# Short filler matmuls: 32 moving columns instead of 512 in TensorE's idle stretches

## The chip, the cores and the metric

The kernel runs on one core of one Trainium2 chip. A core has five engines that run their own instruction lists in order: TensorE (PE: matrix products; its weight loads are listed apart as PEld), VectorE (DVE), ScalarE (ACT), GpSimd (POOL) and SyncE (SP, which here issues the transfers). They meet through semaphores. TensorE writes its results to PSUM banks, from where ScalarE and VectorE read them.

The metric is the device time of one execution in microseconds (us), as the median of several runs. A profile is taken of one more execution, whose own time is given beside its span (first to last instruction).

## The reference: two attentions over one input, mixed by a gate

Input `x` has 2048 tokens of width 640. Two attentions with 32 heads of width 20 are computed from it and mixed token by token.

```python
x = A_x
g = _sigmoid((x * gate_w).sum(-1, keepdims=True))
a = _A_ref(x, A_wqkv, A_wo)      # full attention, softmax over all 2048 keys
b = _B_ref(x, B_wqkv, B_wo)      # 8 keys per token: positions s, s-2, ..., s-14
return g * a + (1 - g) * b
```

Each of the two projects `x` to queries, keys and values, takes a softmax of scaled products, forms the weighted sum of values and projects it with its own `wo`. The full attention takes 32 x 2048 x 2048 exponentials. That is what most of the kernel is about.

## The kernel before: a planned order of work around ScalarE's exponentials

**Tiles and groups.** The full attention runs over 32 groups (`GROUPS`), each a block of 512 queries and four heads. A unit is 128 keys of one head against 512 queries. A step `s` of the main loop takes a tile of two or three units:

- `qk(s)` (line 1992) forms their scores: each unit is a matmul with 32 contracted rows, so the heads of a group lie on four row strips of the array. The scores go to one of two score buffers in PSUM, used in turn.
- `exp(s)` (line 2009) is one ScalarE instruction over 1024 or 1536 columns, from `score` to `ebuf`.
- `pv_slot` calls `pv` (line 2054), which multiplies with the values and accumulates in `obank`, four heads side by side on four column strips of 32.

A part of the exponentials is taken on VectorE and GpSimd in another way (`clamp`, line 1970, reads a score bank into `uD`; lines 1055 and 1086 make shifted copies `eD`; `pv` adds them up). A score matmul for these is called a ride when it comes with a tile, and `lone` issues one by itself.

**Side work.** The projections, the whole local attention (`gen_b`, matmuls at lines 688, 1242 and 1350), the norms and the output projections are generators that are stepped when the main loop leaves room. Their matmuls use three PSUM banks: `side0`, and the third bank of each score buffer when a tile has two units.

**Order.** A planner fixes the order on every engine when the program is built. Each task is added to its engine's list with a planned duration; from these, and a table of latencies `LAT` (0.152 us behind ScalarE, 0.275 us behind TensorE), the planner keeps a planned time for each engine. The times are used only to choose the order. On the chip nothing is left but the lists and the semaphore waits. `PLAN` holds the planner's parameters by step; `FILL` is one of them.

**The edited place.** After `qk`, `exp` and `pv_slot` of a step, `spend(limit, s)` fills TensorE's planned time up to the point where the next step's scores are due. It steps side work, then tries `lone`, and where neither has anything it calls `filler`. That looks at how much of the last 2.3 us of TensorE's planned time is taken (`sch.load(2.3)`). If that is under `FILL` (0.56 to 0.85) it adds one TensorE task: four matmuls on the four column strips, each with a moving operand of 512 columns of `xT` (the input, transposed). They write into a PSUM bank that is free at that time, with the identity as weights, or, if none is, add zero to `obank` with `zero` as weights. Nobody reads what was written to the free bank, and zero added to `obank` changes nothing. The planned duration of the task is 0.215 us. A task waits, as any other, until the bank's last reader is done.

At the start there is a separate run of seven matmuls on zeros (line 584) before the first real work. It is not part of the edit.

Of the kernel before, what the change touches and what calls it, by code (L numbers as in the profile page):

```python
# [415 lines left out]
def _build(ctx, nc, A_x, A_wqkv, A_wo, B_wqkv, B_wo, gate_w, out):  # L416
# [20 lines left out]
    xT = sb([P, CN, S], BF16, "xT")  # L437
# [1623 lines left out]
    def filler(limit):  # L2061

        if sch.load(2.3) >= FILL:
            return False
        best = [b for b in range(NB) if not bank_used[b] and bank_free[b] <= sch.avail["pe"]]
        if best:
            o, w, key = side[best[0]], ident, ("side", best[0])
        elif obank_free <= sch.avail["pe"]:
            o, w, key = obank, zero, "obank"
        else:  # L2070
            return False

        def fn(e):
            for j in range(4):
                ins = e.matmul(o[32 * j:32 * j + 32, :], w[:, 32 * j:32 * j + 32] if best else w[:, :], xT[:, 0, 1536:2048], start=bool(best),
                               stop=bool(best), skip_group_check=True)
            return ins

        t = T("pe", 0.215, fn, reads=["ident" if best else "zero", ("xT", 3, 0, 0), ("xT", 3, 0, 1)], mode="col",
              **({"writes": [key]} if best else {"accum": [key]}))  # L2080
        if best:
            bank_free[best[0]] = t.end
        return True
# [204 lines left out]
```

## Time and profile before

| | before |
|---|---|
| median of 3 runs | 774.17 us (773.98 to 775.07) |
| profiled execution, its own time | 774.52 us |
| its span | 772.7 us |
| mean granted TensorE clock | 0.999 |
| ScalarE busy | 755.7 us (98%) |
| TensorE busy, by its records | 740.4 us (96%) |
| VectorE busy | 695.2 us (90%) |
| GpSimd busy | 343.3 us (44%) |
| matmuls of the edited line | 284, at 112 to 750 us |

How to read the lines of the profile. A group of instructions shows line, engine, operation, destination and source with shapes, count, then busy time and mean duration in ns, then the idle time of the engine just before them and what ended it. A matmul's record lasts longer than the time in which its columns stream, and matmuls on different strips of the array run side by side, so TensorE's busy share is no measure of how full it is. A line of a stretch shows its start and end, its length, then for each engine busy time and count, then the granted TensorE clock as a fraction of full, the DMA share and GB/s. A line of the timeline shows start, length, engine, line, operation and count, and in brackets the idle time before it with its releaser.

### The profile page before, as it was taken

To read this page: it belongs to the slowest core of one execution; us is meant where nothing else is said; L and a number is where in the kernel's file an instruction comes from. 1 tells how busy PE (TensorE), PEld (TensorE's weight loads), DVE (VectorE), ACT (ScalarE), POOL (GpSimd) and SP (SyncE) were. 2 spreads that over 40 slices of the span, in tenths; PEclk is the share of its full clock that TensorE was granted. 3 is DMA by queue.
4 is the path that set the end of the run, shared out by engine and by line. 5 is a ranking of instruction groups with operands and counts; after the bars stand their busy time and mean duration, and the time that the engine had idled before them with its cause. 6 is when DMAs were issued, how large, how long until landed. Compare 5 with 4: busy or idle time off the path is not lost.

```text
span 772.7 us, 30140 instructions
## 1 busy us (share of the span) xinstructions
PE 740.4 (96%) x12398; PEld 290.9 (38%) x12398; DVE 695.2 (90%) x1266; ACT 755.7 (98%) x740; POOL 343.3 (44%) x594
## 2 busy tenths in 40 slices
PE   9999999999999999999999999999999999999998
PEld 6433333232343433334334334433433433343232
DVE  6798988989899899978998989999999999799995
ACT  5999999999999999999999999999999999999996
POOL 4255734635444543334645345343443542442441
PEclk9999999999999999999999999999999999999999
DMA  7321221111121513410124233023112411323201
GB/s 233 118 61 38 48 67 40 35 34 32 37 71 38 121 38 93 115 43 20 36 56 117 53 95 72 27 68 92 42 29 62 104 44 43 89 71 70 69 23 38
DMA packets 71471, 49.89 MB, mean 65 GB/s; under 512 B 43112, under 2 KB 64888, under 8 KB 71336
## 3 DMA queue, kind: packets, MB, share of 16 engines
q1 hardware_dynamic: 70392, 47.54, 24.2%
q8 instruction: 99, 1.62, 0.9%
q10 hardware_dynamic: 944, 0.43, 0.2%
q14 instruction: 36, 0.29, 0.1%
HBM read 32.79 MB, written 7.62 MB: 52 GB/s over the span
## 4 chain that ended last, share of the span: by engine, by line
PE 44%; ACT 31%; issue 14%; DVE 8%; SPq 1%; DMA 1%; POOL 0%; ACTq 0%; DVEq 0%
ACT ebuf L2009 31%; PE score L1992 13%; PE obank L2054 12%; PE side L688 11%; PE score L688 3%; DVE uD L1970 3%; DVE eD L1055 1%; DVE kvw L1338 1%; PE score L1668 1%; DMA woBp<-in_B_wo_dram 1%; DVE kvw L1229 0%; PE side L1350 0%; PE obank L584 0%; PE score L1689 0%; SPq L1032 0%
## 5 line engine op out<-in xcount | busy, mean ns | idle before, releaser
L2009 ACT ACTIVATE ebuf<-score 128x1024 bf16<-128x1024 f32 (+1 forms) x699 | 741.7, 1218 | 3.0 <-PE score L1992 2.2
L1970 DVE TENSOR_SCALAR uD<-score 128x512 int16<-128x512 f32 x427 | 285.5, 682 | 30.5 <-PE score L1992 29.0
L1992 PE MATMUL score<-qT,kT 32*128 32x512 bf16 x1851 | 252.2, 384 | 20.1 <-ACT ebuf L2009 15.7
L1086 POOL TENSOR_TENSOR eD<-uD,two 128x256 int32<-128x256 int32 x299 | 179.8, 615 | 124.3 <-DVE eD L1055 64.4
L1055 DVE TENSOR_SCALAR eD<-uD 128x2048 int16<-128x2048 int16 (+3 forms) x306 | 175.3, 596 | 4.1 <-PE obank L2054 3.3
L2054 PE MATMUL obank<-ebuf,vA 128*21 128x512 bf16 x1616 | 151.7, 385 | 0.1
L1992 PEld LDWEIGHTS score<-qT,kT 32*128 32x128 bf16 x1851 | 62.4, 91 | 212.8 <-ACT ebuf L2009 152.8
L1105 POOL TENSOR_TENSOR vS<-vA,vw 128x252 bf16<-128x252 bf16 x108 | 66.0, 611 | 122.3 <-DVE eD L1055 64.2
L2054 PE MATMUL obank<-eD,vS 128*21 128x512 bf16 x1296 | 110.7, 379 | 0.0
L688 PE MATMUL side<-xT,wBs 128*32 128x256 bf16 x2400 | 95.5, 282 | 1.3 <-DVE qkvB L1167 0.5
L688 PEld LDWEIGHTS side<-xT,wBs 128*32 128x32 bf16 x2400 | 67.8, 142 | 31.5 <-issue 16.1
L1028 POOL TENSOR_TENSOR oN<-oTt,oN 128x256 bf16<-128x256 f32 x60 | 43.8, 730 | 61.1 <-DVE eD L1055 35.5
L2054 PEld LDWEIGHTS obank<-ebuf,vA 128*21 128x21 bf16 x1616 | 36.1, 89 | 80.8 <-issue 58.4
L1338 DVE TENSOR_TENSOR kvw<-kvw,eB 128x2048 bf16<-128x2048 bf16 (+2 forms) x40 | 44.6, 1130 | 0.0
L1229 DVE TENSOR_TENSOR kvw<-qkvB 128x1792 bf16<-128x1792 bf16 (+2 forms) x40 | 43.7, 1126 | 0.2
L2054 PE MATMUL obank<-uD,vA 128*21 128x512 bf16 x432 | 41.9, 379 | 0.0
L1167 DVE CAST qkvB<-side 128x512 bf16<-128x512 f32 (+1 forms) x56 | 36.2, 646 | 3.8 <-PE side L688 3.6
L2054 PEld LDWEIGHTS obank<-eD,vS 128*21 128x21 bf16 x1296 | 31.6, 91 | 19.4 <-issue 2.3
L1013 POOL TENSOR_TENSOR rcp<-rcp,gA 128x16 f32<-128x16 f32 x30 | 7.3, 243 | 60.9 <-DVE eD L1055 28.4
L688 PE MATMUL side<-xT,kvw 128*32 128x512 bf16 (+1 forms) x360 | 30.0, 382 | 0.7 <-DVE vA L914 0.2
L688 PE MATMUL side<-kvw,xT 128*32 128x160 bf16 (+1 forms) x760 | 28.4, 263 | 1.6 <-DVE vA L914 0.8
L1992 PE MATMUL score<-woBp,kT 32*128 32x512 bf16 x192 | 27.2, 384 | 0.6 <-ACT ebuf L2009 0.5
(201 smaller groups left out, 578.7 us busy)
## 6 DMA issues: line engine op xcount, KB each, us to landing
kvw<-scr_v SPq DMA_DIRECT2D x32, 336.5 KB
oN<-scr_n SPq DMA_DIRECT2D x60, 128.0 KB
scr_v<-qkvB SPq DMA_DIRECT2D x32, 85.0 KB
wBs<-in_B_wqkv_dram SPq DMA_DIRECT2D x5, 480.0 KB
WqP<-in_A_wqkv_dram SPq DMA_DIRECT2D x14, 160.0 KB
oTd<-oN SPq DMA_DIRECT2D x108, 20.0 KB
out_dram<-outsb SPq DMA_DIRECT2D x12, 160.0 KB
qT<-dst SPq DMA_DIRECT2D x93, 20.0 KB
```

The lines of the kernel that those rows point to most:

```text
L688: ins = e.matmul(o[j:k, :], l(j) if callable(l) else l[:, j:k], r, start=(first and i == 0), stop=(last and i == n - 1), skip_group_check= ...
L1028: T("pool", 0.73, lambda e, cols=cols: e.tensor_tensor(oN[0][:, cols], oTt[:, cols], rcpR[:, cols], ALU.mult), reads=["oTt", "oN%d" % i], ...
L1055: T("dve", 0.065 + 0.1334 * (n - m), lambda e, k=k, sl=sl, m=m: e.tensor_scalar(eD[:, sl % NS, 512 * m:512 * n].bitcast(I16), uD[d % 2][:, ...
L1086: T("pool", PDUR, lambda e: e.tensor_tensor(eD[:, sl % NS, 512 * i:512 * (i + 1)].bitcast(I32), uD[d % 2][:, 512 * i:512 * (i + 1)].bitcas ...
L1105: T("pool", 0.607, lambda e: e.tensor_tensor(vS[:, d % 2, :, :], _ap(vA, (kb * NQ + q) * 4 * DV, [[0, K - 1], [1, 4 * DV]]), _ap(vw, 0, [[ ...
L1167: t = TB(dvc(n * TOK), lambda e, o=o, i=i: e.tensor_copy(o, i), reads=[("side", b)], writes=[key])
L1229: TB(dvc(n_ * TOK, 2), lambda e: e.tensor_tensor(o, i0, i1, ALU.mult), reads=["qB", "kB"], writes=prods(i, range(n_)) + olds(), port=True)
L1338: TB(dvc(n_ * 2 * TOK, 2), lambda e: e.tensor_tensor(o, i0, i1, ALU.mult), reads=rd, writes=prods(i, range(2 * n_)), port=True)
L1970: t = T("dve", 0.598, lambda e: e.tensor_scalar(uD[d % 2][:, 512 * i:512 * (i + 1)].bitcast(I16), side[x], UOFF, 0.0, op0=ALU.add, op1=ALU ...
L1992: ins = e.matmul(o, kT[32 * j:32 * j + 32, q, kb * P:(kb + 1) * P], qT[qbuf[g]][32 * j:32 * j + 32, :], start=True, stop=True)
L2009: exps[s] = T("act", actc(512 * n), lambda e: e.activation(ebuf[s % NE][:, 0:512 * n], score[s % 2][:, 0:512 * n], ACTF.Exp, scale=LN2 / S ...
L2054: ins = e.matmul(obank[32 * j:32 * j + DV, :], v, src, start=(kb == 0), stop=(last and k >= len(lst) - 4), skip_group_check=True)
```

## The change: 32 columns per filler matmul

Both operand slices of the filler's matmul are cut from 512 to 32 columns: the destination is `o[..., 0:32]` and the moving operand `xT[:, 0, 1536:1568]`. The number of matmuls, their weights, their place in the lists, the banks they wait for and the planned duration of 0.215 us stay, so that the planner makes the same lists in the same order.

```diff
         def fn(e):
             for j in range(4):
-                ins = e.matmul(o[32 * j:32 * j + 32, :], w[:, 32 * j:32 * j + 32] if best else w[:, :], xT[:, 0, 1536:2048], start=bool(best),
+                ins = e.matmul(o[32 * j:32 * j + 32, 0:32], w[:, 32 * j:32 * j + 32] if best else w[:, :], xT[:, 0, 1536:1568], start=bool(best),
                                stop=bool(best), skip_group_check=True)
             return ins
```

## The prediction, made before the changed kernel ran

> **What bounds the kernel now.** I read the page from its top: the busy shares, the chain that ended last, the groups of instructions, and then the same engines over the stretch in which these matmuls run.
>
> ```profile
> span 772.7 us, 30140 instructions
> PE 740.4 (96%) x12398; PEld 290.9 (38%) x12398; DVE 695.2 (90%) x1266; ACT 755.7 (98%) x740; POOL 343.3 (44%) x594
> PE 44%; ACT 31%; issue 14%; DVE 8%; SPq 1%; DMA 1%; POOL 0%; ACTq 0%; DVEq 0%
> L2009 ACT ACTIVATE ebuf<-score 128x1024 bf16<-128x1024 f32 (+1 forms) x699 | 741.7, 1218 | 3.0 <-PE score L1992 2.2
> PEld score L1992 <- ACT ebuf L2009: 171.3, 417, 1.1
> ```
> ```profile
> 20.00:760.00 740.00, 713.27 (x12005) 274.03 (x11997) 677.92 (x1204) 737.25 (x713) 333.65 (x574) 1.00 0.24 60
> 112.00:750.20 638.20, 614.20 (x10245) 237.89 (x10241) 590.47 (x1018) 636.07 (x618) 284.04 (x491) 1.00 0.24 60
> ```
>
> The columns of the second fence are the stretch, its length, then PE, PEld, DVE, ACT and POOL busy, and the granted TensorE clock. ScalarE is the bound: between 112 and 750 us it is busy 636.07 of 638.20 us, and in the whole span its exponentials wait for a score matmul for only 2.2 us. TensorE's 96% hides idleness: its score weight loads wait 171.3 us in total for ScalarE to release a score buffer. So TensorE runs just ahead of ScalarE, and is given the edited matmuls when it has nothing else.
>
> ```profile
> L2075 PE MATMUL obank<-xT,zero x120: 379/379/390, 112.2 to 749.7; 128*32 128x512 bf16 x120
> L2075 PE MATMUL score<-xT,ident x104: 379/379/390, 175.0 to 726.9; 128*32 128x512 bf16 x104
> L2075 PE MATMUL side<-xT,ident x60: 379/379/390, 295.1 to 744.3; 128*32 128x512 bf16 x60
> who waited for it (us, times):
> busy tenths in 40 slices 0000000002102009100020213020011001009770
> L1286 PE MATMUL side<-xT,gwT 128*32 128x64 bf16 x160 | 2.6, 193 | 0.1
> 708.98 1.05 PE L2075 MATMUL side<-xT,ident 128*32 128x512 bf16 x16
> ```
>
> 120+104+60 = 284 matmuls, 71 groups of four that run side by side on four column strips of the array. Nobody waited for one of them: the list behind "who waited for it" is empty. Four groups back to back took 1.05 us, so one group streams for (1.05-0.379)/3 = 0.22 us.
>
> **The change part by part.** *The matmuls become shorter.* No 32-column matmul stands in the trace. Its nearest row is 64 columns, 193 ns; so each group ends at least 379-193 = 186 ns earlier, and at most its 0.22 us of streaming goes. Over 71 groups that is 13.2 to 15.6 us of TensorE time. On the path it is worth nothing that I can see: no consumer waits, the order on every engine, the bank releases and the 284 weight loads are as before, and what comes next on TensorE waits for ScalarE. The cover is ScalarE's own work; its idle time in that stretch, 638.20-636.07 = 2.1 us, is the most that can be gained, if all of it came from these groups. I take 0.
>
> *TensorE becomes idler, and its clock may fall.* This decides. What the trace shows of the clock stands at its two ends. First column: start, length and count for the lines of matmuls; the others are stretches as above.
>
> ```profile
> 1.22 3.17 PE L584 MATMUL obank<-qabs 128*128 128x512 bf16 x7 [1.22 <-DVE qabs L575]
> 4.18 1.27 PE L1668 MATMUL score<-ident,oTd 128*128 128x128 bf16 x10
> 7.35 0.72 PE L1668 MATMUL score<-ident,oTd 128*128 128x128 bf16 x10
> L584 PE MATMUL obank<-qabs 128*128 128x512 bf16 x8 | 3.8, 631 | 1.2 <-DVE qabs L575 1.2
> 768.04 1.07 PE L1467 MATMUL score<-outsb,oN 128*32 128x512 bf16 x20
> 0.04:3.45 3.41, 2.23 (x6) 0.85 (x7) 2.15 (x22) 1.49 (x2) 1.76 (x10) 1.00 0.45 120
> 3.45:6.87 3.42, 3.42 (x25) 2.54 (x24) 0.56 (x1) 0.60 (x1) 2.66 (x3) 1.00 1.02 348
> 769.20:771.40 2.20, 0.00 (x0) 0.00 (x0) 1.15 (x2) 0.04 (x1) 0.00 (x0) 1.00 0.70 244
> 771.50:772.60 1.10, 0.00 (x0) 0.00 (x0) 0.00 (x0) 0.00 (x0) 0.00 (x0) 0.50 0.21 72
> ```
>
> Ten 128-column matmuls took 1.27 us at 4.18 and 0.72 us at 7.35: the clock began at half and doubled some 5.6 us after the first matmul (the 1.00 printed for the first two stretches stands where no clock was recorded yet). At the end it halves at about 771.45, 2.3 us after the last matmul. What judges the activity therefore looks back over something between 2.3 and 5.6 us; I take 3.4 us. [...]
>
> How little activity is enough? I count streaming time at 0.213 to 0.22 us per 512 columns, matmuls side by side once. The last 3.4 us before the fall streamed about 0.78 of 3.41 us, 0.23: too little. At the start, stretch 0.04 to 3.45 had (3.45-1.22)/(3.17-0.631)*6 = 5.3 matmuls of 512 columns, 5.3*0.22/3.41 = 0.34: still half clock; stretch 3.45 to 6.87 was filled at half speed, 0.49: full clock. And the poorest stretches while the clock held:
>
> ```profile
> 204.84:208.25 3.41, 2.28 (x34) 0.59 (x32) 2.99 (x6) 3.41 (x4) 1.32 (x3) 1.00 0.04 8
> 208.25:211.66 3.41, 3.41 (x64) 1.63 (x64) 3.31 (x8) 3.41 (x4) 0.69 (x2) 1.00 0.07 12
> 706.60:710.01 3.41, 2.97 (x44) 0.95 (x41) 3.40 (x5) 3.41 (x4) 0.00 (x0) 1.00 0.47 117
> 710.01:713.43 3.42, 2.96 (x45) 0.83 (x41) 3.15 (x6) 3.42 (x4) 1.85 (x3) 1.00 0.76 179
> ```
> ```profile
> 204.84:208.25 3.41, 0.78 (x8) 0.21 (x8) 1.00 0.04 8
> 706.60:710.01 3.41, 1.71 (x24) 0.54 (x24) 1.00 0.47 117
> ```
> ```profile
> 707.50 0.39 PE L1992 MATMUL score<-qT,kT 32*128 32x512 bf16 x3
> 707.82 0.40 PE L2054 MATMUL obank<-ebuf,vA 128*21 128x512 bf16 x4
> 708.66 0.39 PE L1992 MATMUL score<-qT,kT 32*128 32x512 bf16 x3 [0.44 <-ACT ebuf L2009]
> ```
>
> The second of these fences is the edited line alone: 8 and 24 matmuls, so 2 and 6 groups. Counted over the starts of all 12398 matmuls, the poorest 3.4 us of the whole middle streams 0.46 (at 204.84), and the clock held. Take the streaming out, as the change does: 204.84 falls to 0.34, and 706.60, where between 706.6 and 710 little but the three listed groups and the ends of two others remains, from 0.65 to 0.30. By the same count the next poorest are 0.37 (at 174.1), 0.39 (713.4) and 0.40 (740.7). So if one and the same level raises and drops the clock, it lies between 0.34 and 0.46, and two to five stretches of this execution now fall below it; if dropping takes less than raising, anything down to 0.23 is open. Counting recorded busy time instead, 2.23/3.41 = 0.65 did not raise the clock, 2.28/3.41 = 0.67 kept it, and 204.84 would now have (2.28-2*0.19)/3.41 = 0.56, again below.
>
> *What one fall costs.* For one stretch TensorE streams at half rate. With a demand of d of full speed it ends (2d-1)*3.41 us behind. TensorE is normally ahead of ScalarE by about one exponential less its own reaction:
>
> ```profile
> 711.04 12.04 ACT L2009 ACTIVATE ebuf<-score 128x1024 bf16<-128x1024 f32 x11
> ```
>
> 12.04/11 = 1.09 us, less 0.39 us of score matmul and an estimated 0.3 us of signals (the planner's table `LAT` allows 0.152 us behind ScalarE and 0.275 us behind TensorE, the latter partly inside the record), leaves 0.4 us. The stretch after 204.84 has d = 0.78: 1.9-0.4 = 1.5 us lost by ScalarE, which has no idle time to give it back. After 706.60 d = 0.63: 0.9-0.4 = 0.5 us. After 174.1 d = 0.85: 2.0 us; after 713.4 (0.54) and 740.7 (0.60): 0 and 0.3 us. Two falls cost 2.0 us, five 4.3 us; I take the middle, 3.1 us. Lower bound of the price: 0, if the clock holds. Upper bound: where d is high, a fall costs up to 3.4 us, and every start of a stretch is possible, which gives up to 4 falls a run at the upper level: 4*1.7 = 7 us.
>
> **Sum.** Profiled execution 774.52 us, 0.35 above the median of 774.17: shorter matmuls 0, falls of the clock +3.1, so 777.6 on that execution, 777.3 on the median. I say 777.4.
>
> **The rivals.** *The clock holds.* Dropping may take a level under 0.30, or a full stop: the only fall seen is behind a TensorE that had stopped for good. The longest break in streaming of the middle is 1.03 us by the count of starts, and stays so without the edited streaming; its row is
>
> ```profile
> 205.99 0.39 PE L1992 MATMUL score<-qT,kT 32*128 32x512 bf16 x3 [0.85 <-ACT ebuf L2009]
> ```
>
> with 0.85 us of it outside any record. Then the time is 774.52+0 = 774.2 to 774.5. [...]
>
> *Faster: the groups had been holding up score matmuls.* A group that starts late pushes the next score matmul by up to 0.19 us, and ScalarE with it. It would give up to 774.52-2.1 = 772.4, and it decides once over 1.55 us of ScalarE's 2.1 us come from it. Against it stands the empty list of waiters, and that after such a group the next score matmul usually still waits for ScalarE, as at 708.66 for another group.
>
> *The clock falls and stays down for several stretches.* At half clock no stretch can stream more than 0.5, and with a few waits stays under a level near 0.46. With a mean demand of 0.75 each further stretch costs (1.5-1)*3.41 = 1.7 us; ten give 774.5+17 = 791. Against it: half clock is what fills TensorE, and 0.49 raised it at the start.
>
> **How the numbers follow.** Runs of this kernel spread by 0.14%, so 0.2% (1.55 us) is about what can be told from no change. Short falls of the clock: 0.62, of which 0.55 cost over 0.2% and 0.07 less. A lasting fall: 0.05. The clock holds: 0.25. Faster: 0.08. So faster 0.08, same 0.32, slower 0.60. The likeliest case alone spans 775.8 to 781.5. The range, 773.7 to 781.5, adds the holding clock and leaves out the faster case below and the lasting fall above.
>
> **What would show it.** The edited matmuls at 180 to 193 ns. Granted clock 0.50 in some stretches just behind 204.84, 706.60 or 174.1, with score matmuls of about 0.63 us there (the 631 ns of the half-clock row) and ScalarE idle behind them; ScalarE's wait for score matmuls up from 2.2 us by about the loss. I am wrong if the clock stays at 1.00 throughout; if ScalarE's idle time shrinks instead, the faster rival was right.

## The result, and the profile after

| | before | changed |
|---|---|---|
| median of 22 runs each | 774.48 us (773.87 to 776.68) | 775.64 us (774.26 to 779.16) |
| profiled execution, its own time | 774.52 us | 775.32 us |
| its span, mean granted clock | 772.7 us, 0.999 | 773.5 us, 0.997 |

The ratio over all runs is 1.0019, with a 95% interval of 1.0010 to 1.0028 (the two medians alone give 1.0015): slower beyond the noise, by a little less than the 0.2% that the prediction had named as what can be told from no change. The prediction's 777.4 us was too high. Its range held the time, but its likeliest case began at 775.8 us, just above it.

More telling than the median is how the changed kernel's 22 runs fall apart by their mean granted clock. One stretch of 3.41 us at half clock, as the one at 710.15 below, lowers the mean by 3.41*0.5/773 = 0.0022. The fall behind TensorE's last matmul takes less: the 82 runs of the kernel before that were taken beside the experiments all have 0.999 or 1.000.

| mean clock | runs | times |
|---|---|---|
| 0.998 to 1.000 | 6 | 774.26 to 774.78 us |
| 0.996 to 0.997 | 6 | 774.92 to 776.09 us |
| 0.990 to 0.991 | 5 | 775.60 to 776.29 us |
| 0.987 to 0.988 | 5 | 777.86 to 779.16 us |

Counted in stretches at half clock in the middle, that is one in the first row (none in its one run at 1.000, which took 774.74 us), one or two in the second, four in the third, five or six in the last. The runs of the first row have the time of before, so one such stretch can cost next to nothing. No trace of the changed kernel has more than one; what several cost is read from these times and from the traces of the experiments.

The page of the changed kernel, its span, busy shares, chain, groups of the exponentials and of the score matmuls:

```profile
span 773.5 us, 30140 instructions
PE 731.8 (95%) x12398; PEld 290.2 (38%) x12398; DVE 696.0 (90%) x1266; ACT 756.0 (98%) x740; POOL 343.8 (44%) x594
PE 41%; ACT 34%; issue 17%; DVE 7%; POOL 0%; SPq 0%; ACTq 0%; DMA 0%; DVEq 0%
L2009 ACT ACTIVATE ebuf<-score 128x1024 bf16<-128x1024 f32 (+1 forms) x699 | 742.0, 1218 | 3.4 <-PE score L1992 2.6
L1992 PE MATMUL score<-qT,kT 32*128 32x512 bf16 x1851 | 252.6, 386 | 27.7 <-ACT ebuf L2009 22.4
```

The line of the score matmuls on the page of the kernel before:

```profile
L1992 PE MATMUL score<-qT,kT 32*128 32x512 bf16 x1851 | 252.2, 384 | 20.1 <-ACT ebuf L2009 15.7
```

TensorE's records are 8.6 us shorter in total, and its wait for ScalarE before score matmuls is 22.4 us where it was 15.7: most of the time taken out has become waiting. ScalarE's waiting for score matmuls has grown from 2.2 to 2.6 us; the rest of the 0.8 us between the two profiled executions is within the spread of the runs. The edited line by itself:

```profile
L2075 PE MATMUL obank<-xT,zero x120: 175/179/190, 112.7 to 750.3; 128*32 128x32 bf16 x120
L2075 PE MATMUL score<-xT,ident x104: 176/184/191, 175.5 to 727.7; 128*32 128x32 bf16 x104
L2075 PE MATMUL side<-xT,ident x60: 175/177/191, 295.6 to 745.0; 128*32 128x32 bf16 x60
who waited for it (us, times):
```

Each matmul went from 379 to about 180 ns, and still nobody waits for one. Now stretches of this execution, in the order start and end, length, busy time and count of PE, PEld, DVE, ACT and POOL, then the granted clock:

```profile
204.98:208.39 3.41, 2.15 (x41) 0.69 (x33) 2.63 (x6) 3.41 (x5) 0.97 (x2) 1.00 0.07 14
706.74:710.15 3.41, 2.40 (x45) 0.86 (x38) 3.41 (x5) 3.41 (x4) 0.00 (x0) 1.00 0.45 113
710.15:713.56 3.41, 3.23 (x29) 0.88 (x33) 2.66 (x5) 3.02 (x4) 1.18 (x3) 0.50 0.77 174
713.56:716.97 3.41, 2.49 (x53) 0.89 (x45) 3.41 (x6) 3.41 (x4) 2.02 (x3) 1.00 0.51 102
```

One fall, right behind the stretch at 706.74 that had lost the streaming of six fillers, and for exactly one stretch of 3.41 us. The timeline shows what it did:

```profile
710.33 0.61 PE L1992 MATMUL score<-qT,kT 32*128 32x512 bf16 x3 [0.43 <-ACT ebuf L2009]
710.87 1.04 PE L2054 MATMUL obank<-ebuf,vA 128*21 128x512 bf16 x8
712.26 1.03 PE L1992 MATMUL score<-qT,kT 32*128 32x512 bf16 x6
712.91 1.94 ACT L2009 ACTIVATE ebuf<-score 128x1024 bf16<-128x1024 f32 x2 [0.39 <-PE score L1992]
```

A score matmul takes 0.61 us where it took 0.39, the eight matmuls behind it take 1.04 us, and ScalarE then waits 0.39 us for scores. In the kernel before, its eleven exponentials from 711.04 on, in the line that the prediction shows, follow each other without idle time.

### The profile page after: what moved, and what is told of

Read it like the earlier page. It is cut to its first block, busy times and chain, and to the rows that moved or that the text cites. A ratio compares the mean times of both kernels' runs of the same rounds, so it can differ in the third digit from the quotient of the medians.

```text
span 773.5 us, 30140 instructions
## 1 busy us (share of the span) xinstructions
PE 731.8 (95%) x12398; PEld 290.2 (38%) x12398; DVE 696.0 (90%) x1266; ACT 756.0 (98%) x740; POOL 343.8 (44%) x594
## 4 chain that ended last, share of the span: by engine, by line
PE 41%; ACT 34%; issue 17%; DVE 7%; POOL 0%; SPq 0%; ACTq 0%; DMA 0%; DVEq 0%
ACT ebuf L2009 34%; PE score L1992 13%; PE obank L2054 12%; PE side L688 11%; PE score L688 3%; DVE uD L1970 2%; DVE eD L1055 1%; PE score L1668 1%; PE side L1350 0%; PE obank L584 0%; PE score L1689 0%; DVE kvw L1338 0%; PE side L1242 0%; DVE vA L914 0%; ACT eT L1274 0%
## 5 line engine op out<-in xcount | busy, mean ns | idle before, releaser
L1992 PE MATMUL score<-qT,kT 32*128 32x512 bf16 x1851 | 252.6, 386 | 27.7 <-ACT ebuf L2009 22.4
```

What stands on the lines that cost most here:

```text
L1992: ins = e.matmul(o, kT[32 * j:32 * j + 32, q, kb * P:(kb + 1) * P], qT[qbuf[g]][32 * j:32 * j + 32, :], start=True, stop=True)
```

## The experiments

All kernels keep the lists of every engine in the order of before. Theory A supposes, as the prediction did, that the clock is judged by streaming time, in fixed windows of 3.41 us. Times are compared with the kernel before on the same chip.

**One column strip.** Of each filler's four matmuls only the first is kept, with its 512 columns.

```diff
-            for j in range(4):
+            for j in range(1):
```

> The filler keeps its 512 columns but uses one column strip instead of four, so one matmul of 512 columns in place of four. Theory A (the clock is judged by the time in which columns stream, in fixed windows of 3.41 us, with a level between 0.36 and 0.416): the poorest window streams 0.45 as before, so no fall of the clock in the middle, ratio to before 1.000 (0.999 to 1.001). Rival B (it is judged by the share of the array's cells that work): the poorest windows fall to 0.29, under the 0.33 to 0.35 that would be that theory's level, so 0.5 to 0.8 falls a run, some runs with granted clock of 0.990 or less, ratio 1.001 to 1.002. Rival C (the clock has nothing to do with it; TensorE that finishes its fillers early disturbs the order of events): the fillers end as late as before, so 1.000.

Measured: 774.37 us against 774.53, ratio 0.9999 (0.9990 to 1.0007), and the mean clock is 0.999 to 1.000 in all 11 runs. A quarter of the matmuls, over a quarter of the array's cells, keeps the clock up as the four did. So the share of the array's cells at work, B, is not what is judged: B had expected 0.5 to 0.8 falls a run.

**No fillers.** All 284 matmuls are left out. (The edit would keep one where another engine waits for the task, which is nowhere the case.)

```diff
-            for j in range(4):
+            for j in range(1 if box[0].mark else 0):     # 32 columns where kept
```

> The filler's matmuls are left out altogether (one stays where another engine waits for the task), all lists in the same order. Theory A: the poorest windows stream 0.26, and on the mean over the windows' phase 1.0 to 2.7 falls a run against 0.6 to 1.9 with 32 columns; so the ratio is 1.002 to 1.006, runs without a fall at the time of before. Rival B: 2.5 to 3.2 falls, 1.004 to 1.008. Rival C, and a judge that counts issued matmuls instead of columns: much worse than the 32-column filler, since 284 instructions are gone (a judge of instructions), or better than it (if the fillers' weight loads had cost something).

Measured: 778.93 us against 774.53, ratio 1.0053 (1.0036 to 1.0069), mean clock 0.987 to 0.991 in all 6 runs. So it is worse than with 32 columns, by more stretches at half clock, as A said (B's range holds the ratio too). Its profile shows that a fall can last:

```profile
294.76:298.17 3.41, 2.11 (x29) 0.67 (x25) 3.41 (x6) 3.41 (x5) 2.52 (x5) 1.00 0.52 137
298.17:301.58 3.41, 3.41 (x29) 0.71 (x29) 3.41 (x5) 3.41 (x3) 0.37 (x1) 0.50 0.07 15
711.18:721.42 10.24, 9.07 (x72) 1.80 (x72) 7.38 (x12) 9.52 (x10) 2.28 (x4) 0.50 0.41 88
```

From 711.18 the clock stays down for 10.24 us, three times 3.41. The fall at 298.17 cost ScalarE nothing there (busy 3.41 of 3.41 us), though TensorE was busy throughout.

**128 and 256 columns.** The filler's width alone, here for 128:

```diff
-                ins = e.matmul(o[32 * j:32 * j + 32, :], ..., xT[:, 0, 1536:2048], ...
+                ins = e.matmul(o[32 * j:32 * j + 32, 0:128], ..., xT[:, 0, 1536:1536 + 128], ...
```

> The filler moves 128 columns. Theory A: the poorest window streams 0.366; 0 to 0.7 falls a run, at the 174, 204 and 740 us stretches first, no longer at 706; median equal to before within 0.1%, a few runs 1 to 3 us longer. Rival B: about the same, 0.5 to 0.8. Rival C: in proportion to columns, three quarters of the loss with 32 columns in every run: ratio 1.0015.

> The filler moves 256 columns. Theory A: the poorest window streams 0.40; under 0.1 falls a run, ratio 1.000. Rival B: under 0.1, 1.000. Rival C: half the loss of 32 columns, ratio 1.001. If runs with a granted clock under 0.995 are seen, the level lies above 0.41 and theory A's bracket is too low.

Measured: 128 columns 774.71 us, ratio 1.0004 (0.9995 to 1.0013); 256 columns 774.63 us, ratio 0.9999 (0.9991 to 1.0008), both against 774.53. A cost in proportion to the columns taken away (C) would have been 1.0015 and 1.001 by the ratio measured for 32 columns; both lie just outside the intervals, though by the lower end of that ratio's own interval they would not. With 256 columns the mean clock is 0.998 or more in all runs, with 128 it is so in ten of eleven. The profiled run with 128 columns had the fall at 204, and so its price:

```profile
205.05:208.46 3.41, 1.95 (x36) 0.69 (x33) 3.02 (x7) 3.41 (x4) 1.50 (x3) 1.00 0.04 8
208.46:211.87 3.41, 3.41 (x41) 1.12 (x38) 2.63 (x8) 2.63 (x3) 0.51 (x2) 0.50 0.07 12
L2009 ACT ACTIVATE ebuf<-score 128x1024 bf16<-128x1024 f32 (+1 forms) x6 | 6.9, 1275 | 1.2 <-PE score L1992 1.2
```

The last line is ScalarE alone between 208 and 214 us: 1.2 us idle, all for score matmuls.

**One place at a time.** 32 columns only in the fillers at 174 to 208 us (5 of 71), at 706 to 719 us (15) or at 743 to 750 us (8), counted in the order in which they are placed; then the other way round, 512 columns in these 28 and 32 in the other 43.

```diff
+        nfil[0] += 1
+        wf = 32 if nfil[0] in range(47, 62) else 512
```

> 32 columns only in the five fillers at 174 to 208 us, 512 in the other 66. Theory A (windows of 3.41 us, level about 0.39 of streaming): 0.3 falls a run, at most two, granted clock not under 0.995; from the prediction's working 2.0 us for a fall behind 174 and 1.5 us behind 204; a test of these two prices, as runs without a fall must have the time of before. Rival D (a fall costs what its place says less well than how many falls come close together, so only the group at 706 to 720 us is dear): under 1 us for each fall here.

> 32 columns only in the fifteen fillers at 706 to 719 us. Theory A: 0.5 falls a run, up to two or three in one run, as the windows after a fall are poor themselves (0.31 and 0.36 at half clock did not bring the clock back without fillers); prediction's price 0.5 us for the fall behind 706 and 0 behind 713. Rival D: this group carries most of the loss of the changed kernel: runs with falls 1.5 to 4 us longer, the ratio about 1.0015.

> 32 columns only in the eight fillers at 743 to 750 us. Theory A: 0.3 falls a run, 0.3 us each by the prediction's working; ratio 1.000, clocks of 0.995 to 0.998 in a third of the runs. Rival D: the same number of falls, and a cost under 1 us.

> 512 columns in the 28 fillers at 174 to 208, 706 to 719 and 743 to 750 us, 32 in the other 43. Theory A: the poorest window streams 0.41, just over the level, so no fall, ratio 1.000 (0.999 to 1.001): a short filler costs nothing by itself. Rival C (shorter fillers cost time by themselves, in proportion to their number): 43 of 71, 60% of the loss, ratio 1.001 with the clock at 1.00.

| 32 columns at | median, before 774.41 us | ratio (95%) | mean clock |
|---|---|---|---|
| 174 to 208 | 774.61 us | 1.0006 (0.9997 to 1.0016) | 9 of 11 runs 0.999 to 1.000; 0.998 (775.88 us), 0.995 (777.83 us) |
| 706 to 719 | 775.67 us | 1.0014 (1.0005 to 1.0023) | one run 1.000 (773.64 us), the others 0.992 to 0.996 |
| 743 to 750 | 774.97 us | 1.0010 (1.0000 to 1.0019) | 7 runs 0.999 to 1.000 (774.20 to 775.09 us), 4 runs 0.997 to 0.998 (775.63 to 777.11 us) |
| the other 43 | 774.25 us | 1.0001 (0.9993 to 1.0010) | 5 runs 0.999 to 1.000, 6 runs 0.997 to 0.998 |

The group at 706 to 719 falls in nearly every run, and so carries the largest part of the median. D, that a fall elsewhere costs under 1 us, is wrong: the run with 0.995 in the first row is over 3 us longer than its neighbours without a fall, with two falls, and the four runs with a fall at 743 are 1.9 us longer on the mean than the seven. Their profiled run had one fall, at 745.02. Its stretches, and ScalarE alone between 745 and 753 us:

```profile
741.60:745.01 3.41, 2.07 (x49) 0.83 (x49) 3.41 (x5) 3.41 (x4) 1.07 (x2) 1.00 0.00 0
745.02:748.43 3.41, 3.41 (x30) 0.71 (x27) 2.12 (x4) 2.67 (x3) 0.60 (x1) 0.50 0.02 5
L2009 ACT ACTIVATE ebuf<-score 128x1536 bf16<-128x1536 f32 (+1 forms) x6 | 7.6, 1332 | 1.3 <-PE side L1992 0.7 <-PE score L1992 0.5
```

The last row of the table has A's time but not its clock: no fall was expected, and six runs, at 0.997 and 0.998, have one. In the profiled run, at 0.997, it is at 298.11. It cost ScalarE nothing: its next wait for scores is 0.49 us at 329.73, and one like it stands at 329.15 in the trace with 32 columns at 174 to 208, whose clock stayed at 1.000. The two stretches and the wait, then the other trace's wait:

```profile
294.69:298.10 3.41, 2.48 (x42) 0.80 (x34) 3.41 (x6) 3.41 (x5) 2.52 (x5) 1.00 0.42 116
298.11:301.51 3.40, 3.35 (x37) 1.04 (x37) 3.40 (x5) 3.39 (x3) 0.42 (x1) 0.50 0.06 13
329.73 2.85 ACT L2009 ACTIVATE ebuf<-score 128x1024 bf16<-128x1024 f32 x3 [0.49 <-PE score L1992]
```
```profile
329.15 3.77 ACT L2009 ACTIVATE ebuf<-score 128x1024 bf16<-128x1024 f32 x4 [0.46 <-PE score L1992]
```

So a stretch that streams 0.41 of its time (here and below by a count over the starts of all matmuls) can fall, and in the run with 706 to 719 one with 0.46 fell:

```profile
707.63:711.04 3.41, 2.35 (x42) 0.81 (x46) 3.41 (x5) 3.41 (x3) 0.69 (x2) 1.00 0.42 113
711.05:714.46 3.41, 3.10 (x33) 0.69 (x25) 3.22 (x5) 3.24 (x4) 1.78 (x3) 0.50 0.90 193
```

while the stretch at 204.98 of the changed kernel, with 0.42, had kept the clock. Streaming time, then, is not what is judged. In the stretches that fell although they streamed much, much of the streaming is of score matmuls, each of which feeds 32 rows of the array where the others feed 128 (32*128 against 128*21 and 128*32 in the lines of the timelines).

**One row strip.** The filler becomes one matmul of 512 columns on one column strip, as in the first experiment, but with 32 contracted rows instead of 128.

```diff
-            for j in range(4):
-                ins = e.matmul(o[32 * j:32 * j + 32, :], ..., xT[:, 0, 1536:2048], ...
+            ins = e.matmul(o[0:32, :], w[0:32, 0:32], xT[0:32, 0, 1536:2048], ...
```

> One matmul of 512 columns per filler, on one column strip as in the one-strip run, but with 32 contracted rows instead of 128: it streams as long, over a quarter of the array's rows. Theory A (streaming time of any matmul counts, level about 0.39): poorest window 0.45, no fall, ratio 1.000. Theory A2, formed from the windows of the runs so far (what counts is the share of the array's rows that are fed, so a score matmul of 32 rows counts a quarter; one level of about 0.365 both ways): poorest window 0.30, about 1.0 fall a run, by the grid's position none to three, granted clocks of 0.990 to 0.997 in about half the runs, mean time 0.5 to 1 us over before, runs without a fall at the time of before.

Measured: mean clock 1.000 in 4 of 10 runs, 0.991 to 0.998 in six, of which the profiled one, at 0.998, has one fall. The clock falls, as A2 said and A did not. The time, 776.86 us against 774.42, ratio 1.0035 (1.0020 to 1.0050), can't be used in full: its four runs at a clock of 1.000 take 774.81 to 775.91 us, so this filler seems to cost something besides the clock. Its profiled run fell behind 204.78:

```profile
204.78:208.19 3.41, 2.45 (x31) 0.70 (x27) 2.86 (x6) 3.41 (x4) 1.19 (x3) 1.00 0.05 11
208.20:211.60 3.40, 3.40 (x39) 1.20 (x38) 2.50 (x7) 2.93 (x4) 0.81 (x3) 0.50 0.07 12
```

TensorE is busy by its records for 2.45 us of the stretch that fell, against 2.15 us of the changed kernel's stretch at 204.98, which kept the clock; so recorded busy time, the prediction's other count, isn't what is judged either. The TensorE lines of the first, then those of the second:

```profile
204.81 0.39 PE L1992 MATMUL score<-qT,kT 32*128 32x512 bf16 x3
206.06 0.39 PE L1992 MATMUL score<-qT,kT 32*128 32x512 bf16 x3 [0.86 <-ACT ebuf L2009]
206.38 0.40 PE L2054 MATMUL obank<-ebuf,vA 128*21 128x512 bf16 x4
206.61 0.39 PE L2054 MATMUL obank<-uD,vA 128*21 128x512 bf16 x4
206.93 0.38 PE L2074 MATMUL obank<-xT,zero 32*32 32x512 bf16 x1
207.41 0.39 PE L1992 MATMUL score<-qT,kT 32*128 32x512 bf16 x3
207.73 0.24 PE L857 MATMUL side<-woBp,KMd 128*32 128x128 bf16 x4
207.80 0.23 PE L857 MATMUL side<-qabs,KMd 128*32 128x128 bf16 x4
207.96 0.40 PE L2074 MATMUL score<-xT,ident 32*32 32x512 bf16 x1
```
```profile
204.91 0.39 PE L2054 MATMUL obank<-eD,vS 128*21 128x512 bf16 x4
205.23 0.39 PE L1992 MATMUL score<-qT,kT 32*128 32x512 bf16 x3
206.49 0.39 PE L1992 MATMUL score<-qT,kT 32*128 32x512 bf16 x3 [0.86 <-ACT ebuf L2009]
206.81 0.40 PE L2054 MATMUL obank<-ebuf,vA 128*21 128x512 bf16 x4
207.03 0.39 PE L2054 MATMUL obank<-uD,vA 128*21 128x512 bf16 x4
207.25 0.19 PE L2075 MATMUL obank<-xT,zero 128*32 128x32 bf16 x4
207.83 0.39 PE L1992 MATMUL score<-qT,kT 32*128 32x512 bf16 x3 [0.40 <-ACT ebuf L2009]
208.15 0.24 PE L857 MATMUL side<-woBp,KMd 128*32 128x128 bf16 x4
208.22 0.23 PE L857 MATMUL side<-qabs,KMd 128*32 128x128 bf16 x4
```

At 0.213 us per 512 columns (in the trace of before, matmuls of line 584 start 0.427 us apart at half clock; half of that) the first streams 3 + 2 + 2 groups and two short ones, 7*0.213+0.11 = 1.60 us, 0.47 of the stretch. The second streams the end of one group (0.14), 3 + 2 groups, two short ones and a little: 1.35 us, 0.40 (the count over starts gave 0.42; the two ways differ by up to 0.02). The one that streams more is the one that fell. Weighed by rows fed, a score group of three units counts three quarters, and the 32-row filler one quarter: 3*0.16+2*0.21+0.11+2*0.05 = 1.11 us, 0.33, fell; 0.14+3*0.16+2*0.21+0.11+0.03 = 1.18 us, 0.35, kept.

Two points that near to each other don't make a level. The same counts, from the starts of all matmuls in the windows of all twelve traces, with that of the next run, give (at half clock the counts are halved):

| share of the window | highest that lost the clock | lowest that kept it |
|---|---|---|
| streaming, any matmul | 0.49 (one row strip, 204.8) | 0.38 (32 at 706 to 719, 769.1) |
| cells of the array at work | 0.36 (no fillers, 707.8) | 0.33 (one row strip, 716.8) |
| rows of the array fed | 0.37 (no fillers, 707.8) | 0.36 (changed, 205.0) |

A level divides best by rows fed: the two sides overlap by 0.01, against 0.03 and 0.11. By rows, a half clock stayed at up to 0.36 and was raised from 0.34 or 0.37 on, depending on how the starts at half clock are counted. So a single level of about 0.36, both ways, fits all windows to within 0.02, which is what the counting of streaming from starts may well miss. The experiments showed that rows count (one row strip: mean clock 0.991 to 0.998 in six of 10 runs) and that columns of the array don't (one column strip: 0.999 to 1.000 in all 11); that nothing else does, and the level itself, are read from these windows and were not tested further.

**The changed kernel once more**, for a trace with another position of the windows.

> The changed kernel once more, to have a trace with another position of the windows. Theory A2 gives, on the mean over positions, 2.4 falls a run: none or one in about half the positions, up to five in the others, behind 174, 204, 294, 706, 713 and 740 us. Prices by the prediction: 2.0 us behind 174, 1.5 behind 204, 0.5 behind 706, 0 behind 713, 0.3 behind 740, to be read as ScalarE's new idle time behind each.

Measured: 776.56 us against 774.42, ratio 1.0029 (1.0014 to 1.0043), over 8 runs with mean clocks from 0.998 (774.75 us) to 0.985 (780.39 us). The profiled one is the former, with one fall in the middle, at 712.37, for which ScalarE waits 0.38 us at 714.17:

```profile
708.95:712.36 3.41, 2.26 (x40) 0.70 (x34) 3.41 (x5) 3.41 (x4) 1.41 (x3) 1.00 0.50 113
712.37:715.78 3.41, 3.41 (x40) 0.97 (x37) 2.33 (x5) 3.03 (x4) 1.78 (x3) 0.50 0.79 168
```

The fall behind 174 was in no trace, so its price stays unmeasured by itself.

## Why the prediction was right in direction and too high in size

- **Shorter matmuls are worth nothing on the path: right.** They became 200 ns shorter, more than the 186 ns taken. The one run at full clock takes 774.74 us, the time of before, and with 43 short fillers the five runs at 0.999 to 1.000 take 773.40 to 774.96 us. TensorE waits for ScalarE instead. The faster rival is out.
- **A stretch of 3.41 us: right.** The 3.41 in the prices was a choice between 2.3 and 5.6 us that no line of the profile before fixed more closely. The falls of the later traces bear it out: 3.41 us each (3.413 in the changed kernel's clock record, from 710.149 on), or 10.24, three times that.
- **The clock falls behind the poorest stretches: right,** with score matmuls of 0.61 us (0.63 was said), at 0.50, behind 706.60 and, in traces of other kernels of the series, behind 204.8 to 205.1 and 741.6. Behind 174.1 and 713.4 no trace has a fresh fall.
- **The level: the right neighbourhood by the wrong quantity.** Streaming time, with a level between 0.34 and 0.46, could not have told that 0.41 at 294 and 0.46 at 707 fall and 0.42 at 205 doesn't. The stretch at 294 was missing from the prediction's list for that reason. The prediction had held one level for both directions to be an assumption; by rows one level of about 0.36 fits the windows to within 0.02.
- **"Two falls cost 2.0 us, five 4.3 us; I take the middle, 3.1 us": this is the step that failed,** in both of its factors. The number: it was read off one position of the windows, that of the profiled execution, with some 3.5 falls in the middle of two and five. The prediction did say that every start of a stretch is possible, but used it for the upper bound alone; a window that straddles a poor stretch and a full one may not fall. Twelve of 22 runs have none to two stretches at half clock. The 22 mean clocks give 2.7 on the mean (lost clock times the span, by 1.7 us a stretch, less 0.2 for the end, as in the 82 runs of before); counted by rows over all positions it is 2.4. The price: 3.1 us is 0.9 us a fall. The mean time of the 22 runs is 1.4 us above that of before, 0.5 us a stretch. Of the missing 1.7 us (3.1 against 1.4) the number explains about 0.7, the price 1.0. The median lies lower still, 1.2 us up.
- **The price by place: right for some, wrong for others.** Predicted 0.5 us behind 706, measured 0.4 twice; 1.5 behind 204, measured 1.2 twice; 0.3 behind 740, measured 1.3. Behind 294, which the prediction did not list, two falls cost nothing. So cheap places missing from the list lowered the mean, and one place was dearer than the formula. Why it was so at 745 was not tested; the flat 0.4 us of lead may be what is wrong there. The 0.3 us of signals in that lead is the planner's figure, and no run shows it. In the trace of before, the 43 groups of score matmuls for which TensorE had waited on ScalarE start 0.06 us behind the end of the exponential, and the six exponentials that had waited for scores start 0.04 to 0.05 us behind the end of the score matmuls.
- **The clock holds:** this happens in one of 22 runs, by the counts as a matter of the windows' position. As a property of the kernel it is refuted. Nor does a fall need a long break: in the stretch from 204.78 with one row strip, behind which the clock fell, the longest wait is 0.86 us.
- **A fall that lasts:** it was given 0.05, at 1.7 us for each further stretch. Without fillers, and with short ones at 706 to 719, the clock does stay down for three stretches, since 711 to 718 is poor at half clock too. But all three together cost ScalarE 1.2 us, so 0.4 us a stretch instead of 1.7: work that is poor enough to keep the clock down also asks little of TensorE. No trace of the changed kernel itself shows such a fall.
- **The chances:** short falls that cost under 0.2%, which is what came, had been given 0.07, against 0.55 for dearer ones. That the range held the time owes something to its lower part, which had been added for a clock that holds.

## What to carry to other kernels

Work without effect can be worth its time on an engine that isn't the bound, where the clock depends on it, as it did here: 778.93 us at mean clocks of 0.987 to 0.991 without the fillers, 774.53 us at 0.999 to 1.000 with them. Its worth is shown by the granted clock of many runs, not by the busy share of one. What told the stretches of this kernel apart was how much of the array's rows is fed in 3.41 us: fillers were needed only where that share got down to some 0.37, the highest that lost the clock, and matmuls with 32 contracted rows counted little for it. When an effect depends on where windows fall that lie differently from one execution to the next (in the two traces of the changed kernel a fall began at 710.15 and at 712.37), work out its mean over their positions, and take the one execution that was profiled as one draw.

## What the runs showed of the hardware that was not expected

- The clock's changes lie on one grid for the whole run: every fall seen in the middle lasted one or three times 3.41 us (10.24 us without fillers), and full clock lasted 764.585 us in the profile before, 764.585/224 = 3.4133, and 703.146 us up to the fall of the changed kernel, 703.146/206 = 3.4133. That the clock is judged in such windows is read from these lengths.
- A matmul on one column strip of 32, with all 128 rows fed, held the clock as four side by side did: 71 instead of 284 matmuls, clock 0.999 to 1.000 in 11 runs. It saved no time here (0.9999).
- A filler of 32 rows by 32 columns seems to cost time beyond the clock. Its four runs at full clock are up to 1.5 us longer than the median of before, and TensorE's idle time ahead of it that no wait explains is 7.4 us over 28 times, against 3.2 us over 14 for the changed kernel's fillers. Whether that idle time is what costs, and why it is there, was not tried. The lines are from the views of the filler's line, first the one-row-strip kernel, then the changed one (us, times):

```profile
  issue: 7.4, 28
```
```profile
  issue: 3.2, 14
```
